# Loading batch 0's queries and keys by halves of the tokens, in sixteen transfers from two queues

## The chip, the core and the metric

One core of a Trainium2 chip runs the whole kernel. Its engines are TensorE (PE in the profile, with its weight loads as PEld), VectorE (DVE), ScalarE (ACT), GpSimd (POOL) and SyncE (SP); the rows SPq are SP's own DMA queue. Transfers between the main memory and the core's on-chip memory are carried out by 16 DMA engines. The metric is the device time of one execution in microseconds (us); of the kernel before there are three such times, and their median counts.

## The reference, cut to what matters

Blockwise causal attention (8 batches, 8 heads, 576 tokens, head size 64; a block of 64 queries sees its own and all earlier key blocks), whose output is the input of a channel mix with a shift by one token:

```python
scores = scale * np.matmul(q, k.transpose(0, 1, 3, 2))
scores = np.where(block_i >= block_j, scores, -1e9)
attn = np.exp(scores - scores.max(-1)); attn /= attn.sum(-1) + 1e-9
x = np.matmul(attn, v).transpose(0, 2, 1, 3).reshape(B, S, H * D)     # 8 x 576 x 512
x_prev = x shifted by one token, zeros first
xk = mu_k * x + (1 - mu_k) * x_prev;  xr = mu_r * x + (1 - mu_r) * x_prev
out = sigmoid(xr @ w_r) * (np.maximum(xk @ w_k, 0) ** 2 @ w_v)        # 512 -> 1024 -> 512
```

## The kernel before, in words

The kernel is written as a list of 958 tasks. Each task belongs to one engine and issues a few instructions. Three hand-held tables set everything: `ORDER` is the order in which all tasks are issued (and so the order on each engine; `+5` behind a number puts five matmuls of 512 columns that nobody reads in front of that PE task, line L256), `PLACE` gives for each task with a choice the engine that does it (A, D or P), and `RINGS` gives the number of buffers of each kind. Engines run their own list in order and wait for each other through semaphores.

The tasks, by the names that the text uses:

- `qkld b g n`: SP loads the queries (n = 0) or keys (n = 1) of four heads (g = 0 or 1) of batch b into one of the six load buffers `t_ld`, 128 x 1152 float32, 576 KB. Heads are numbered 4g + 2x + y. A partition holds nine consecutive tokens of one head of each x; y picks the upper or the lower 64 partitions.
- `qk b g n`: a cast to bf16 into `t_nl` (POOL, DVE or ACT, L247 or L243), which puts the two x side by side.
- `turn b g n`: nine 128 x 128 transposes on PE (L350) into a score buffer `t_s` in PSUM, three of which exist; `ev b g n` copies it to `t_qkt`, where a batch's queries and keys lie with the head size on the partitions.
- `sc b part i`: the matmuls of one score unit (L422), and `ex b part i` its exponential on ACT (L431). Batch 0 is cut in two: part 0 is tokens 0 to 255 with three units, part 1 tokens 256 to 575 with ten. Later batches have twelve units.
- `av b part S` sums the exponentials (L470, L481), `av b part A` and `B` multiply them with the values `t_vo` (L497); then `t1`, `rec`, `t2` and `norm` on DVE divide, `d` (L622) takes the difference to the token before, and `mul` (L639) writes the mixed inputs XK and XR.
- `pk`, `pr`, `pv` are the three matrix products of the channel mix on PE (L686 and, for its first chunk by halves, L706; L731; L760), over nine chunks of 512 tokens. `relu`, `sq`, `tanh` and `o` lie between and behind them, and SP stores.

The channel mix needs the mixed inputs of tokens, and so attention of batch 0 has to be through before the first `pk` can run. Weights go through the same six load buffers: they are loaded behind batch 0's queries and keys. Batches 4 to 7 turn their queries and keys by DMA transposes and are not touched.

Of the kernel before, what the change touches and what calls it, by code (L numbers as in the profile page):

```python
# [21 lines left out]


ORDER = """
# [50 lines left out]
"""  # L75


PLACE = (
    "AAPDAPDADDDAAADADAPDDDDDPPPAPAPAPDDDPDDDAAPAPAAAPPDPPDDAPADDDDDDPD"
    "DPDPAPPPPPPPDPPPPPPPDPDPAADDPDPPAADPPADADPDAADDDDDDAAPDPAPAAAADPAA"  # L80
    "APDPAADPDPAADAAADPDPDDDAADADAPAPAADPDPAAADAPAAADDAADDDDDAPAPAPAPDA"
    "ADAPAPDPAAAADDAPADAPDAADADDDADADADAAAPAPADADADADADADAD"
)


# [67 lines left out]
def kernel(  # L153
# [12 lines left out]
    nc = tc.nc  # L166
    B, H, S, D = q.shape
# [7 lines left out]
    QC = 32  # L175
    JT = S // D
    HALF = S // 2
# [34 lines left out]
    def new(buf):  # L212
        return slots[buf["ring"], buf["slot"]]
# [44 lines left out]
                identb[:, :].unsqueeze(1).to_broadcast([P, 4, P]),  # L258
                start=True, stop=True)

    def load(key, buf, jobs):
        def fn(eng, me):
            for dst, src in jobs(new(buf)):
                nc.sync.dma_start(dst, src)
        return add(key, "SP", fn, uses=[buf])

    cast, ready, evac = {}, {}, {}
    vo_buf = [plan.buf("vo") for _ in range(B)]
    qkt_buf = [plan.buf("qkt") for _ in range(B)]
# [3 lines left out]
    def halves(ld, w):  # L273
        return ld[:, 0:2 * w].rearrange("p (x e) -> p x e", x=2)
# [32 lines left out]
                                 AD if name == "v" else ANY, fn, [t], [ld])  # L307


    def where(n, g, y, lo):  # L310

        return ((g * 2 + n) * 2 + y) * S + lo

    def add_qk(b, g, n):
        src = (q, k)[n]
        ld, nl = plan.buf("ld"), plan.buf("nl")
        cross = b in CROSS
        if cross:
            t = load(f"xld {b} {g} {n}", ld, lambda d: [
                (d[:, :].rearrange("p (t d) -> p t d", d=D),  # L320
                 src[b, 4 * g:4 * g + 4].rearrange(
                     "h s d -> (h s) d").rearrange("(t p) d -> p t d", p=P))])
        else:
            t = load(f"qkld {b} {g} {n}", ld, lambda d: [
                (halves(d, S), src[b, 4 * g:4 * g + 4].rearrange(
                     "(x y) (p j) d -> (y p) x (j d)", y=2, j=JT))])

        def fn(eng, me):
            return convert(
                eng, new(nl)[:, :].rearrange("p (t x d) -> p x t d", x=2, d=D),  # L330
                new(ld)[:, :].rearrange("p (x t d) -> p x t d", x=2, d=D))
        c = add(f"qk {b} {g} {n}", ANY, fn, [t], [ld, nl])
        at = where(n, g, 0, 0)
        if cross:
            def turn(eng, me):
                nc.sync.dma_start_transpose(
                    out=new(qkt_buf[b])[:, at:at + 2 * S].rearrange(
                        "p (t c) -> p t c", c=P),
                    in_=new(nl)[:, 0:2 * S])
            evac[b, g, n] = add(f"xturn {b} {g} {n}", "SP", turn, [c],  # L340
                                [nl, qkt_buf[b]])
            return
        m = plan.buf("s")

        def turn(eng, me):
            unread(me, new(m)[:, 0])
            pst = new(m)[:, :, :].rearrange("p a b -> p (a b)").bitcast(BF)
            for j in range(JT):
                at = slice(j * P, (j + 1) * P)
                nc.tensor.matmul(pst[:, at], new(nl)[:, at], identb,  # L350
                                 is_transpose=True, start=True, stop=True)
        t = add(f"turn {b} {g} {n}", "PE", turn, [c],
                [nl, m, qkt_buf[b]])

        def ev(eng, me):
            pst = new(m)[:, :, :].rearrange("p a b -> p (a b)").bitcast(BF)
            convert(eng, new(qkt_buf[b])[:, at:at + 2 * S].rearrange(
                "q (p j) -> q p j", j=JT),
                pst[:, 0:2 * S].rearrange("q (j p) -> q p j", p=P))
        evac[b, g, n] = add(f"ev {b} {g} {n}", AD, ev, [t],  # L360
                            [m, qkt_buf[b]])

# [43 lines left out]
    def add_scores(key):  # L406
# [6 lines left out]
        def fn(eng, me):  # L413
            qkt, PS = new(qkt_buf[b]), new(m)
            unread(me, PS[:, 0])
            for y, t, col, q0, n in pieces:
                for g in range(2):
                    for x in range(2):
# [4 lines left out]
                            PS[g * D:g * D + D, x, col:col + n],  # L423
                            qkt[rows, ka:ka + D], qkt[rows, qa:qa + n],
                            start=True, stop=True)
        deps = [evac[b, g, n] for g in range(2) for n in range(2)]
        pe = add(f"sc {b} {part} {i}", "PE", fn, deps,
                 [m, qkt_buf[b], ebuf[key]])

# [418 lines left out]
```

## Time and profile before

| | |
|---|---|
| median of three executions | 256.73 us (255.5 to 257.11) |
| profiled execution | 255.6 us, of which the profile's span is 253.3 us |
| busy time in the span | PE 241.4 us, DVE 193.6, ACT 172.4, POOL 83.2 |
| granted TensorE clock | full (9 tenths or more in all 40 slices) |
| chain that ended last | PE 75%, DVE 10%, ACT 7%, DMA 3%, issue 2% |
| moved by DMA | 48.21 MB, 190 GB/s on average |

The profile is of one execution; times in it count from the start of its span. PE's busy time counts the unread matmuls of L256 as well, and pipelined matmuls overlap in it. The chain is followed back from the last instruction to whatever released each step. A view by windows gives the busy time of each engine, the share of time in which the 16 DMA engines were at work, and the bytes that they moved in any stretch.

### The profile page before, as it was taken

What the parts mean: (1) busy time and instruction counts of PE and PEld (TensorE: products, weight loads), DVE (VectorE), ACT (ScalarE), POOL (GpSimd) and SP (SyncE); (2) the same over time, 40 slices, a digit from 0 to 9 for tenths busy, and PEclk for the clock granted to TensorE, in tenths of its full rate; (3) what the DMA queues carried; (4) which work ended last, traced back from release to release, by engine and by line L of the source; (5) the groups of instructions that cost most, each with busy time, mean ns of one, the idle gap of its engine ahead of it and who ended that gap; (6) DMA issues with size and microseconds to landing.
All of it is one profiled execution on the core that took longest, in us unless ns stands there. A gap on an engine that the chain in (4) does not pass through costs nothing.

```text
span 253.3 us, 7859 instructions
## 1 busy us (share of the span) xinstructions
PE 241.4 (95%) x3429; PEld 125.8 (50%) x3429; DVE 193.6 (76%) x274; ACT 172.4 (68%) x228; POOL 83.2 (33%) x74
## 2 busy tenths in 40 slices
PE   4999599999999999999999999999999999999994
PEld 2555474774464444644554455445544554444452
DVE  1348898899999999889836979998798579943532
ACT  3699599989988369558595958597549931450630
POOL 1033523433543453651578001335750043010100
PEclk9999999999999999999999999999999999999999
DMA  7999998999999999999999999979913002203103
GB/s 238 297 290 400 372 284 215 323 270 175 278 260 181 211 231 222 184 215 217 192 225 192 224 229 232 211 196 196 177 44 124 3 3 83 87 0 126 39 21 145
DMA packets 105905, 48.21 MB, mean 190 GB/s; under 512 B 94736, under 2 KB 94992, under 8 KB 105872
## 3 DMA queue, kind: packets, MB, share of 16 engines
q1 hardware_dynamic: 105872, 47.72, 81.1%
q8 instruction: 26, 0.43, 0.7%
q14 instruction: 7, 0.06, 0.1%
HBM read 33.56 MB, written 9.44 MB: 170 GB/s over the span
## 4 chain that ended last, share of the span: by engine, by line
PE 75%; DVE 10%; ACT 7%; DMA 3%; issue 2%; POOL 0%; DVEq 0%; ACTq 0%; POOLq 0%
PE t_mm L760 24%; PE t_mm L686 19%; PE t_mm L731 11%; PE t_s L497 7%; ACT t_e L431 6%; PE t_s L422 6%; PE t_s L481 4%; PE t_s L350 2%; DMA t_ld<-in_moe_w_v_dram 2%; DVE XK L639 2%; PE t_mm L256 2%; DMA t_ld<-in_k_dram 1%; DVE t_xt L595 1%; DVE t_d L622 1%; DVE XR L639 1%
## 5 line engine op out<-in xcount | busy, mean ns | idle before, releaser
L431 ACT ACTIVATE t_e<-t_s 128x1024 f16<-128x1024 f32 (+2 forms) x97 | 87.4, 977 | 10.2 <-PE t_s L422 10.1
L760 PE MATMUL t_mm<-WV,t_k 128*128 128x512 f16 (+1 forms) x296 | 65.8, 374 | 0.1
L686 PE MATMUL t_mm<-XK,WK 128*128 128x512 f16 x256 | 60.3, 379 | 0.4 <-DVE t_kr L666 0.2
L674 POOL TENSOR_TENSOR t_k<-t_kr 128x512 f16<-128x512 f32 x26 | 27.2, 1059 | 72.7 <-DVE t_k L674 31.0
L664 ACT ACTIVATE t_kr<-t_mm 128x512 f32<-128x512 f32 x48 | 28.7, 603 | 24.6 <-PE t_mm L686 23.2
L760 PEld LDWEIGHTS <-t_k 128*128 128x128 f16 x296 | 27.7, 98 | 32.5 <-issue 1.5
L686 PEld LDWEIGHTS <-WK 128*128 128x128 f16 x256 | 23.8, 97 | 30.0 <-issue 4.4
L768 DVE SCALAR_TENSOR_TENSOR t_o<-t_t,t_mm 128x512 f32<-128x512 f32 (+1 forms) x37 | 24.6, 667 | 16.1 <-PE t_mm L760 14.9
L740 ACT ACTIVATE t_t<-t_mm 128x512 f32<-128x512 f32 x36 | 21.6, 606 | 21.0 <-PE t_mm L731 20.7
L731 PE MATMUL t_mm<-WR,XR 128*128 128x512 f16 x144 | 35.6, 380 | 0.1
L639 DVE SCALAR_TENSOR_TENSOR XK<-t_d,MU,t_xt 128x576 f16<-128x576 f32 (+4 forms) x44 | 31.3, 739 | 0.0
L639 DVE SCALAR_TENSOR_TENSOR XR<-t_d,MU,t_xt 128x576 f16<-128x576 f32 (+4 forms) x44 | 31.0, 725 | 0.0
L422 PE MATMUL t_s<-t_qkt 64*64 64x64 bf16 (+7 forms) x672 | 29.1, 284 | 0.8 <-ACT t_e L431 0.4
L622 POOL TENSOR_TENSOR t_d<-t_xt 128x1152 f32<-128x1152 f32 (+1 forms) x10 | 19.3, 1937 | 24.7 <-DVE t_xt L595 13.3
L247 POOL CAST t_nl<-t_ld 128x1152 bf16<-128x1152 f32 x14 | 15.9, 1144 | 33.2 <-DMA t_ld<-in_k_dram 14.3
L674 DVE TENSOR_TENSOR t_k<-t_kr 128x512 f16<-128x512 f32 x27 | 19.3, 726 | 9.6 <-ACT t_kr L664 9.2
L497 PE MATMUL t_s<-t_e,t_vo 64*32 64x320 f16 (+7 forms) x1344 | 23.8, 278 | 2.4 <-issue 2.3
L422 PEld LDWEIGHTS <-t_qkt 64*64 64x64 bf16 x672 | 15.3, 106 | 19.5 <-issue 16.0
L247 POOL CAST t_vo<-t_ld 64x1152 f16<-64x1152 f32 x16 | 18.5, 1154 | 19.8 <-DVE t_d L622 8.1
L497 PEld LDWEIGHTS <-t_vo 64*32 64x32 f16 x1344 | 17.9, 92 | 9.9 <-issue 5.2
L666 DVE TENSOR_SCALAR t_kr<-t_mm 128x512 f32<-128x512 f32 x24 | 16.2, 686 | 6.7 <-PE t_mm L686 6.4
L731 PEld LDWEIGHTS <-XR 128*128 128x128 f16 x144 | 13.2, 98 | 15.3 <-issue 1.3
(44 smaller groups left out, 197.4 us busy)
## 6 DMA issues: line engine op xcount, KB each, us to landing
t_ld<-in_k_dram SPq DMA_DIRECT2D x16, 576.0 KB, 7.1
t_ld<-in_q_dram SPq DMA_DIRECT2D x16, 576.0 KB, 6.4
t_ld<-in_v_dram SPq DMA_DIRECT2D x16, 576.0 KB, 7.4
out_dram<-t_o SPq DMA_DIRECT2D x35, 256.0 KB, 2.4
t_ld<-in_moe_w_k_dram SPq DMA_DIRECT2D x4, 512.0 KB, 7.9
t_ld<-in_moe_w_v_dram SPq DMA_DIRECT2D x4, 512.0 KB, 5.5
t_ld<-in_moe_w_r_dram SPq DMA_DIRECT2D x2, 512.0 KB, 6.8
t_qkt<-t_nl SPq DMA_TRANSPOSE x16, 4.5
```

What stands on the lines that cost most here:

```text
L247: return e.tensor_copy(dst, src)
L422: nc.tensor.matmul(PS[g * D:g * D + D, x, col:col + n], qkt[rows, ka:ka + D], qkt[rows, qa:qa + n], start=True, stop=True)
L431: nc.scalar.activation(new(ebuf[key])[:, :, 0:width], new(m)[:, :, 0:width], AF.Exp, scale=ISQ)
L497: nc.tensor.matmul(dst(slice(c * QC, (c + 1) * QC), u, f, q0, n), weights(b, u, c, t, f), new(ebuf[key])[u * D:u * D + D, x, col:col + n], ...
L622: return e.tensor_tensor(new(d)[:, 0:2 * n].rearrange("p (u t) -> p u t", u=2), x[:, :, 1 + lo:1 + hi], x[:, :, lo:hi], ALU.subtract)
L639: return nc.vector.scalar_tensor_tensor((XK, XR)[kr][:, cc, g:g + w], new(d)[:, u * n + at - lo:u * n + at - lo + w], MU1[:, kr, cc:cc + 1 ...
L664: nc.scalar.activation(new(kr), new(m), AF.Relu)
L674: return e.tensor_tensor(dst(), KR, KR, ALU.mult)
L686: nc.tensor.matmul(ps, WK[:, cc, jc * P:(jc + 1) * P], XK[:, cc, at:at + CH], start=(cc == 0), stop=(cc == CCn - 1))
L731: nc.tensor.matmul(ps, XR[:, cc, g % R:g % R + P], WR[:, cc], start=(cc == 0), stop=(cc == CCn - 1))
L760: nc.tensor.matmul(ps[:, 0:w], k2[:, jc, jt * P:(jt + 1) * P], WV[:, jc, cols], start=(jc == 0), stop=(jc == JCn - 1))
L768: nc.vector.scalar_tensor_tensor(new(o)[:, 0:w], new(tb)[:, cols], 1.0, new(m)[:, 0:w], ALU.add, ALU.mult)
```

## The change

For batch 0 alone, n is now a half of the tokens (n = 0: tokens 0 to 287, n = 1: 288 to 575), and one load buffer holds both tensors: queries in partitions 0 to 63, keys in 64 to 127. A buffer is filled by four transfers: for each pair of heads x and each tensor one, with 64 destination partitions of 2,304 bytes. Their source is two heads y, 36,864 elements apart, with 32 runs of 576 elements each. The n = 0 buffers take the two tensors by two queues (queries from SP, keys from ACT), the n = 1 buffers all from SP. The cast and the nine transposes stay as they were; the copy behind the transposes spreads its columns over the four places (queries and keys, y = 0 and 1). The three score units of part 0 wait for the two n = 0 copies only; part 1 waits for all four. `ORDER` and `PLACE` are new throughout; the unread matmuls are 25 instead of 33.

```diff
 ORDER = """
-26 34 22 30 0 41 27 28+5 35 29 36+2 37 23 24+4 25 116 31 38 1 32+4 33 76+5
+30 22 34 31 26 32+5 23 38 33 24+2 25 35 48+5 44 41 49 36 27 45 46 37 47 28+1
...
-    def load(key, buf, jobs):
+    def load(key, buf, jobs, also=None):
         def fn(eng, me):
-            for dst, src in jobs(new(buf)):
-                nc.sync.dma_start(dst, src)
+            for n, (dst, src) in enumerate(jobs(new(buf))):
+                (nc.sync if n % 2 == 0 or also is None else also).dma_start(
+                    dst, src)
         return add(key, "SP", fn, uses=[buf])
...
-        else:
+        elif b:
             t = load(f"qkld {b} {g} {n}", ld, lambda d: [
                 (halves(d, S), src[b, 4 * g:4 * g + 4].rearrange(
                     "(x y) (p j) d -> (y p) x (j d)", y=2, j=JT))])
+        else:
+            t = load(f"qkld {b} {g} {n}", ld, lambda d: [
+                (halves(d, S)[i * D:(i + 1) * D, x],
+                 a[0, 4 * g + 2 * x:4 * g + 2 * x + 2,
+                   n * HALF:(n + 1) * HALF].rearrange(
+                       "y (r j) d -> y r (j d)", j=JT))
+                for x in range(2) for i, a in enumerate((q, k))],
+                None if n else nc.scalar)
...
         def ev(eng, me):
             pst = new(m)[:, :, :].rearrange("p a b -> p (a b)").bitcast(BF)
+            if not b:
+                convert(eng, new(qkt_buf[0])[:, g * 4 * S:(g + 1) * 4 * S]
+                        .rearrange("q (a t) -> q a t", a=4)[
+                            :, :, n * HALF:(n + 1) * HALF].rearrange(
+                                "q a (r j) -> q a r j", j=JT),
+                        pst[:, 0:2 * S].rearrange(
+                            "q (j a r) -> q a r j", a=4, r=QC))
+                return
...
-        deps = [evac[b, g, n] for g in range(2) for n in range(2)]
+        deps = [evac[b, g, n] for g in range(2)
+                for n in range(1 if (b, part) == (0, 0) else 2)]
```

SP's queue at the program's start, before; `t_ld_58` to `t_ld_63` are the six load buffers:

```order
L264 DMA t_ld_58<-in_k_dram 128x2x576
L264 DMA t_ld_59<-in_k_dram 128x2x576
L264 DMA t_ld_60<-in_q_dram 128x2x576
L264 DMA t_ld_61<-in_q_dram 128x2x576
L279 DMA MU<-in_moe_mu_k_dram 128x2x2
L279 DMA MU<-in_moe_mu_r_dram 128x2x2
L264 DMA t_ld_62<-in_v_dram 128x18x64
L264 DMA t_ld_63<-in_k_dram 128x2x576
```

The same place after, with the semaphores that an issue waits for; DMAHW0 to DMAHW7 are the eight semaphores that transfers count up when they have landed, given out in turn to SP's and ACT's transfers:

```order
L264 DMA t_ld_58<-in_q_dram 64x1x576 x2
L264 DMA t_ld_59<-in_q_dram 64x1x576 x2
L264 DMA t_ld_60<-in_q_dram 64x1x576 [waits DMAHW0_49]
L264 DMA t_ld_60<-in_k_dram 64x1x576 [waits DMAHW1_49]
L264 DMA t_ld_60<-in_q_dram 64x1x576 [waits DMAHW2_49]
L264 DMA t_ld_60<-in_k_dram 64x1x576 [waits DMAHW3_49]
L264 DMA t_ld_61<-in_q_dram 64x1x576 [waits DMAHW4_49]
L264 DMA t_ld_61<-in_k_dram 64x1x576 [waits DMAHW5_49]
L264 DMA t_ld_61<-in_q_dram 64x1x576 [waits DMAHW6_49]
L264 DMA t_ld_61<-in_k_dram 64x1x576 [waits DMAHW7_49]
L264 DMA t_ld_62<-in_v_dram 128x18x64 [waits DMAHW0_49]
L264 DMA t_ld_63<-in_v_dram 128x18x64 [waits DMAHW1_49]
```

Four loads of all 128 partitions have become twelve transfers here (and four more on ACT); from the ninth transfer on, each issue waits until an earlier one has landed, and the values, mu and everything else stand behind them.

ACT at the program's start, before (`t_s_150` to `t_s_152` are the three score buffers, `t_e` the exponentials):

```order
L243 ACT_TABLE_LOAD
L243 CAST t_nl_67<-t_ld_58 128x2x9x64
L243 COPY t_qkt_74<-t_s_150 128x1152
L243 COPY t_qkt_74<-t_s_151 128x1152
L243 COPY t_qkt_74<-t_s_152 128x1152
L431 ACTIVATE t_e_84<-t_s_151 128x1024
L431 ACTIVATE t_e_86<-t_s_150 128x1024
L431 ACTIVATE t_e_87<-t_s_151 128x2x256
```

And after:

```order
L264 DMA t_ld_58<-in_k_dram 64x1x576 x2
L264 DMA t_ld_59<-in_k_dram 64x1x576 x2
L243 ACT_TABLE_LOAD
L243 COPY t_qkt_74<-t_s_151 128x4x288
L452 ACTIVATE t_e_84<-t_s_152 128x2x256
L452 ACTIVATE t_e_85<-t_s_150 128x1024
L452 ACTIVATE t_e_86<-t_s_152 128x1024
L243 CAST t_vo_79<-t_ld_62 64x18x64
L452 ACTIVATE t_e_87<-t_s_151 128x1024
```

ACT issues four of the transfers first, does one of the four copies instead of all of them, and has the three exponentials of part 0 ahead of the values' cast and the ten of part 1.

More of the change, by code (lines that the diff above doesn't have):

```diff
@@ L24 @@
 ORDER = """
[50 rows of a table removed]
[50 rows of a table added]
 """
 PLACE = (
[L79 to L82, printed above, removed]
+    "APAPPPAADADADDPDDDADDDDPDDPAPADDAADPPDDPDAPAAAAADAPPDDPDPAPADAAADA"
+    "PPDPAADAADDPDPPDAPAADPDPAAADAPPDDDDPPPDPDPDAADADDDAAADADDPDPDADPDP"
+    "DADDDDDDAPAPDDADAPAPDAAADADPDAAAAPAADADDADDDADAPDAADDDDAADDPADDPDP"
+    "DPADDPDPDPDPDPDADDDDAAADADADADADAPADADADAPADAPADADADAD"
 )
```

98 rows, old and new, of the table ORDER are left out of this document.

## The prediction

> **What bounds the kernel now.** I read the page first, then the windows, the chain in order of time, the timeline of the first 40 us, and the DMA views of the same stretch. The page says that PE is busy nearly throughout and closes the chain:
>
> ```profile
> PE 241.4 (95%) x3429; PEld 125.8 (50%) x3429; DVE 193.6 (76%) x274; ACT 172.4 (68%) x228; POOL 83.2 (33%) x74
> PE 75%; DVE 10%; ACT 7%; DMA 3%; issue 2%; POOL 0%; DVEq 0%; ACTq 0%; POOLq 0%
> ```
>
> The windows say where PE is not the bound. First three rows of all instructions, then two of the unread matmuls of L256 alone (columns: stretch, length, PE busy, PEld busy, and so on, DMA share and GB/s last):
>
> ```profile
> 20.00:30.00 10.00, 6.34 (x224) 4.26 (x223) 8.29 (x18) 7.21 (x9) 3.69 (x4) 1.00 1.04 394
> 30.00:40.00 10.00, 9.80 (x187) 6.83 (x185) 9.23 (x17) 9.59 (x12) 2.97 (x3) 1.00 1.09 276
> 120.00:240.00 120.00, 120.00 (x1544) 58.43 (x1543) 91.90 (x125) 75.85 (x108) 38.51 (x30) 1.00 0.64 137
> 0.00:10.00 10.00, 5.09 (x11) 1.41 (x11) 1.00 0.83 264
> 10.00:20.00 10.00, 5.01 (x19) 1.45 (x19) 1.00 1.13 299
> ```
>
> From 30 us on PE has work all the time; from 120 to 240 it is busy in all of it. Before 30 us half of PE's busy time is unread matmuls, and from 20 to 30 it stands 3.7 us. So the kernel is a start of 30 us, set by batch 0, and then a stretch in which PE works off a fixed list. Whatever moves the end of the start moves the end of the kernel by as much, less what PE has done ahead. The start is read in the timeline:
>
> ```profile
> 4.28 1.15 ACT L243 CAST t_nl<-t_ld 128x1152 bf16<-128x1152 f32 x1 [2.27 <-DMA t_ld<-in_k_dram]
> 9.99 0.76 DVE L247 CAST t_nl<-t_ld 128x1152 bf16<-128x1152 f32 x1 [1.02 <-DMA t_ld<-in_q_dram]
> 11.16 0.67 PE L350 MATMUL t_s<-identb,t_nl 128*128 128x128 bf16 x9
> 11.86 1.12 ACT L243 COPY t_qkt<-t_s 128x1152 bf16<-128x1152 bf16 x1 [0.25 <-PE t_s L350]
> 12.83 1.05 PE L422 MATMUL t_s<-t_qkt 64*64 64x320 bf16 x32
> 13.47 10.63 ACT L431 ACTIVATE t_e<-t_s 128x1024 f16<-128x1024 f32 x13 [0.49 <-PE t_s L422]
> 30.21 1.04 PE L706 MATMUL t_mm<-XK,WK 128*128 128x256 f16 x8
> ```
>
> The first cast starts when the first load has landed (4.28), the last when the fourth has (9.99). 2.84 us later the first scores run, then 13 exponentials back to back until 24.10, and the first `pk` at 30.21. The loads come at the speed of the DMA engines, all 16 busy:
>
> ```profile
> 0.00:2.30 2.30, 1.00 0.17 26
> 2.30:10.00 7.70, 5.88 (x32) 3.21 (x31) 1.53 (x3) 3.39 (x3) 0.00 (x0) 1.00 1.02 335
> 2.30:4.30 2.00, 1.38 (x4) 0.19 (x2) 0.00 (x0) 0.02 (x1) 0.00 (x0) 1.00 1.00 385
> 20.00:25.00 5.00, 4.53 (x170) 2.92 (x169) 3.85 (x7) 4.95 (x7) 2.19 (x2) 1.00 1.05 395
> ```
>
> Nothing flows before 2.3 us; then a DMA share of 1.00 to 1.05 goes with 335 to 395 GB/s, that is 20.9 to 24.7 GB/s for one engine of 16.
>
> **The change, part by part.**
>
> *The bytes* are the same: 16 transfers of 64 runs of 2,304 bytes are 2.36 MB, as four loads of 576 KB.
>
> *On how many engines they run* decides all. Each load of before had an outermost count of 128 on the on-chip side, and its source could be merged into evenly spaced rows: 64 rows of 576 elements are just the 36,864 elements from one head to the next. The new source cannot: 32 runs cover 18,432 elements, then the next head starts 36,864 after the first. So its outermost count is two. If a transfer is dealt to the engines by its outermost count, as 128 rows fall into 16 equal shares, there are only two shares here. If the 2 x 32 runs are counted as 64 first, there are 16. No row of before shows a transfer with such a source; the ends are 2 engines and 16. I take 2, because the pattern as it stands has no even stride over its 64 runs, and all rows that show 16 belong to patterns that do.
>
> The Trainium skill, DMA: Bandwidth & Descriptors, section "Why a DMA increments its semaphore by 16 and not by 1", says the same more sharply: the engines used are the largest number up to 16 that divides the outermost count (not 1) of both patterns, and the lowest-numbered ones, for SP and ACT alike; counts of 2 and 64 give two. No run here shows it yet. The page's 27 GiB/s for one engine would give, as an estimate, 41 us for the 2.36 MB and 285 us in all by the sum below.
>
> *The price by two engines.* 24.4 GB/s (385 to 395 over 16) times two is 48.8 GB/s, and 2.36 MB take 48.4 us: the last lands at 2.3 + 48.4 = 50.7 us. The n = 0 buffers, half of the bytes, land by 26.5. Issuing does not add to it: an issue takes about half a microsecond of SP,
>
> ```profile
> 0.73 0.97 SPq L264 DMA_DIRECT2D t_ld<-in_k_dram  x2
> L264 SPq DMA_DIRECT2D t_ld<-in_moe_w_k_dram x4: 545/551/3450, 10.6 to 20.1; - x4
> ```
>
> and transfers nine to sixteen wait for the first eight, while those keep the two engines busy. Behind them on SP's queue stand the values, mu, batch 1's loads and, through the six buffers, the weights. Their shares on the two engines lie behind the small transfers too, so all of them come late by about the same.
>
> *Behind the last landing* comes the old tail: 2.84 us to the scores, with one difference, the copy on DVE instead of ACT (+0.24):
>
> ```profile
> L247 DVE COPY t_qkt<-t_s 128x1152 bf16<-128x1152 bf16 x3 | 4.0, 1348 | 3.6 <-PE t_s L350 3.6
> L243 ACT COPY t_qkt<-t_s 128x1152 bf16<-128x1152 bf16 x13 | 14.3, 1120 | 6.8 <-PE t_s L350 6.8
> ```
>
> So part 1's scores run at 50.7 + 2.84 + 0.24 = 53.8, and its exponentials from 54.4 (0.64 later, as at 12.83 and 13.47). The new copy has more dimensions; I price it as the old one, since it is as many elements with the same stride, and twice its time would add 1.35.
>
> *What the split gains:* part 0's three exponentials are done in the wait for n = 1. They are 2,560 of 11,520 columns, so 2.4 of the 10.63 us. The ten others take 8.3 and end at 62.7, against 24.10 before: 38.6 later.
>
> *To the first `pk`* it was 6.1 us from there. Now ACT has, behind the ten, a copy, a cast, two copies and a weight cast to do:
>
> ```profile
> L243 ACT CAST t_nl<-t_ld 128x1152 bf16<-128x1152 f32 x8 | 9.1, 1157 | 5.0 <-DMA t_ld<-in_k_dram 4.5 <-issue 0.5
> L243 ACT CAST WK<-t_ld 128x1024 f16<-128x1024 f32 x2 | 2.1, 1046 | 0.4 <-DMA t_ld<-in_moe_w_k_dram 0.4
> ```
>
> 3 x 1.12 + 1.16 + 1.05 = 5.6, so `pk` at 68.3, 38.1 later. By then PE has done one turn and two score units of batch 1 more than at 30.21 (0.5 and 0.35 each in the chain):
>
> ```profile
> 71.94 0.50 PE t_s L350 x9
> 43.74 0.37 PE t_s L422 x4
> ```
>
> That is 1.2 us of its fixed list. The eight unread matmuls that were dropped lay in idle time and give nothing.
>
> *The rest of the order.* Ten `relu`, seven `sq`, three casts, two copies and three `d` go to DVE, some casts leave it; by the order's counts and the rows' durations that is some 15 us more on DVE and as much less on POOL:
>
> ```profile
> L666 DVE TENSOR_SCALAR t_kr<-t_mm 128x512 f32<-128x512 f32 x24 | 16.2, 686 | 6.7 <-PE t_mm L686 6.4 <-PE t_mm L706 0.2
> L674 DVE TENSOR_TENSOR t_k<-t_kr 128x512 f16<-128x512 f32 x27 | 19.3, 726 | 9.6 <-ACT t_kr L664 9.2
> 40.00:60.00 20.00, 19.17 (x375) 12.22 (x377) 17.27 (x24) 17.80 (x23) 8.75 (x8) 1.00 1.00 267
> 60.00:90.00 30.00, 29.49 (x436) 15.17 (x428) 28.46 (x35) 22.49 (x30) 11.90 (x10) 1.00 1.14 221
> ```
>
> PE's bound hides it while DVE has room: 28 us are free in 120 to 240, only 4.3 in 40 to 90. If half of it fell in there, 3.3 us would stick out. I take 0 and keep 3 for the range.
>
> *Sum:* 38.1 - 1.2 = 36.9 on the profiled execution's 255.6, 292.5. That execution is 1.1 below the median of the three, 256.73, within their spread of 1.6. I forecast **293 us**.
>
> Its own range: at 20.9 GB/s an engine the last lands at 58.7, 8 later; at the fastest slice of the loads, 430 GB/s over 16 or 26.9 an engine, at 46.2, 4.5 earlier:
>
> ```profile
> GB/s 0 0 0 0 0 0 146 131 338 399 392 422 400 399 430 369 376 284 215 307 361 399 384 392 392 307 353 363 223 187 196 246 290 286 286 237 212 166 187 338
> ```
>
> That is 288 to 301, with 3 to 4 for the order 285 to 305.
>
> **The rivals.**
>
> *Sixteen engines after all (not slower).* Place: the first transfers; the mechanism is a deal over 64 runs. The first buffer lands near 4.3, the second near 6; SP issues n = 1 after that, four and four at 0.55 each, and the last lands near 11.3 (8.9 for the last issue, 2.4 for a quarter of the first load's bytes). That is 39.4 before my 50.7: 253.5 us, faster by 1.2%. For it: weights with differing patterns on both sides run at 395 GB/s. Against it: their counts divide by 16 on both sides. It decides where the last lands before 50.7 - 36.9 = 13.8, at 205 GB/s, eight or nine engines.
>
> *Each queue on two engines of its own.* Then SP's and ACT's n = 0 transfers run beside each other and land by 14.4; the eight of n = 1, all SP's, take 24.2 more: 38.6, 12.1 earlier than forecast, 281 us. For it: two queues; against it: nothing in the trace shows queues that own engines, since with SP alone all 16 were busy.
>
> The Trainium skill, same page, "Issuing engines are not separate DMA queues", says that a second issuing engine saves only issue time; no run here shows it yet.
>
> *Sixteen engines, but DVE binds* where it was nearly full, from 40 to 90: 253.5 + 3.3 = 257, no change. For it the window rows; against it that the work comes from POOL, which is idle two thirds of the span, so that the new order need not put it into that stretch.
>
> **How the numbers follow.** Two engines 0.83, four 0.05, sixteen 0.09, sixteen with DVE bound 0.03. The likeliest gives 293. For 8 in 10 I go from 279, which takes in the four engines, to 306. 1%, 2.6 us, is about what a measurement of this kernel can tell from no change: the first two cases are slower; sixteen engines is mostly over 1% faster, and DVE's case within it. Faster 0.07, same 0.05, slower 0.88.
>
> **What would show it.** Right: a low DMA share (about 0.13) and some 50 GB/s until about 50 us; the first cast at about 14 us, not 4; part 0's exponentials near 30 us, part 1's not before 54; PE with long waits up to 68 us and full from there. Wrong: a DMA share near 1.0 with over 300 GB/s in the first 10 us, and exponentials of part 0 at 9 to 10 us; then the whole sum falls. If the transfers are slow but the end is far from 293, the rate of an engine or the later order was mis-sized, which the windows behind the first `pk` would tell.

## The result, and the profile after

| | before | after |
|---|---|---|
| median of four executions each | 256.36 us (255.5 to 257.11) | 293.65 us (292.52 to 294.78) |
| profiled execution, and its span | 255.6 us, 253.3 | 293.86 us, 291.1 |
| first `pk` in the profile | 30.21 us | 68.69 us |

The ratio of the times is 1.1456, 95% interval 1.1396 to 1.1516. The forecast was 293 us, with a range of 279 to 306. The times below leave out an execution that lies over 1.5% above the fastest of the same kernel; there was one such, 261.33 us in the run with one transfer for each head.

The page of the profile after: busy times; the granted clock, the DMA share and the GB/s in 40 slices of 7.3 us each; and the chain by engine.

```profile
PE 243.3 (84%) x3421; PEld 125.3 (43%) x3421; DVE 203.7 (70%) x292; ACT 173.5 (60%) x222; POOL 68.8 (24%) x62
PEclk9999855799999999999999999999999999999999
DMA  0111141999969999999989899999997600111103
GB/s 30 52 51 51 52 112 54 237 378 311 314 223 329 263 305 196 214 225 178 236 177 263 160 183 239 199 152 240 207 219 145 189 3 2 74 72 72 72 6 140
PE 66%; SPq 12%; ACT 6%; DMA 6%; DVE 4%; issue 4%; POOL 1%; POOLq 0%; DVEq 0%; ACTq 0%
```

PE is busy 243.3 us, 1.9 more than before, in a span that is 37.8 longer: nearly all the new time is standing time. SP's queue and the DMAs, the latter 3% of the chain before, have 18% of it. The DMA row does not rise above 1 tenth in the first five slices, to 36 us, where the rate stays at 30 to 52 GB/s.

Windows of the profile after (stretch, length, busy time of PE, PEld, DVE, ACT and POOL, granted clock, DMA share, GB/s):

```profile
2.30:10.00 7.70, 1.37 (x4) 0.18 (x2) 0.00 (x0) 1.28 (x1) 0.00 (x0) 1.00 0.13 46
10.00:20.00 10.00, 1.93 (x11) 1.09 (x11) 0.00 (x0) 0.00 (x0) 1.14 (x1) 1.00 0.13 51
30.00:40.00 10.00, 2.31 (x31) 1.29 (x29) 0.76 (x1) 1.51 (x2) 0.00 (x0) 0.71 0.13 52
40.00:50.00 10.00, 1.24 (x15) 0.47 (x13) 0.00 (x0) 1.02 (x1) 0.00 (x0) 0.50 0.44 99
60.00:70.00 10.00, 8.46 (x210) 5.82 (x208) 9.82 (x19) 9.77 (x11) 3.37 (x4) 1.00 1.02 369
70.00:291.00 221.00, 216.20 (x2996) 109.97 (x2988) 182.91 (x255) 152.71 (x200) 62.48 (x51) 1.00 0.81 177
```

The first 7.7 us of the loads, which had a DMA share of 1.02 and 335 GB/s, have 0.13 and 46. 0.13 is two engines of 16, and it stays there to 40 us. From 40 to 50 the values come in beside them, and from 60 to 70, with the weights and batch 1, it is 1.02 and 369 GB/s. The last 221 us of the kernel before, for the last row:

```profile
32.00:253.00 221.00, 216.58 (x3002) 110.68 (x3000) 177.30 (x240) 150.14 (x205) 74.80 (x61) 1.00 0.80 172
```

PE does 0.4 us less in it, DVE 5.6 more, POOL 12.3 less. So the new order left the late part as long as it was: the lost time is all in the start.

The start in the timeline of the profile after (start, duration, engine, line, operation; in brackets the idle time before and what ended it):

```profile
0.73 12.51 SPq L264 DMA_DIRECT2D t_ld<-in_q_dram  x5
16.87 1.14 POOL L247 CAST t_nl<-t_ld 128x1152 bf16<-128x1152 f32 x1 [15.57 <-DMA t_ld<-in_q_dram]
18.07 1.14 PE L360 MATMUL t_s<-identb,t_nl 128*128 128x128 bf16 x9 [14.40 <-POOL t_nl L247]
26.70 0.76 DVE L247 CAST t_nl<-t_ld 128x1152 bf16<-128x1152 f32 x1 [25.45 <-DMA t_ld<-in_q_dram]
27.38 1.35 DVE L247 COPY t_qkt<-t_s 128x1152 bf16<-128x1152 bf16 x1
31.14 1.51 ACT L452 ACTIVATE t_e<-t_s 128x512 f16<-128x512 f32 x2 [1.32 <-PE t_s L441]
38.17 0.76 DVE L247 CAST t_nl<-t_ld 128x1152 bf16<-128x1152 f32 x1 [9.44 <-DMA t_ld<-in_k_dram]
40.76 1.02 ACT L452 ACTIVATE t_e<-t_s 128x1024 f16<-128x1024 f32 x1 [8.10 <-PE t_s L441]
50.52 0.76 DVE L247 CAST t_nl<-t_ld 128x1152 bf16<-128x1152 f32 x1 [11.59 <-DMA t_ld<-in_k_dram]
55.06 8.21 ACT L452 ACTIVATE t_e<-t_s 128x1024 f16<-128x1024 f32 x10 [1.56 <-PE t_s L441]
68.69 1.05 PE L727 MATMUL t_mm<-XK,WK 128*128 128x256 f16 x8 [0.33 <-ACT WK L243]
```

Each of the four casts ends an idle time of its engine of 9 to 25 us, with a transfer as what ended it. The fourth can start at 50.52, against 9.99 before. From there to the first `pk` it is 18.2 us, against 20.2 before, with three of the exponentials already done.

### The profile page after: what moved, and what is told of

It is laid out like the page before. It is cut to its first block, busy times and chain, and to the rows that moved or that the text cites. A ratio compares the mean times of both kernels' runs of the same rounds, so it can differ in the third digit from the quotient of the medians.

```text
span 291.1 us, 7877 instructions
## 1 busy us (share of the span) xinstructions
PE 243.3 (84%) x3421; PEld 125.3 (43%) x3421; DVE 203.7 (70%) x292; ACT 173.5 (60%) x222; POOL 68.8 (24%) x62
## 4 chain that ended last, share of the span: by engine, by line
PE 66%; SPq 12%; ACT 6%; DMA 6%; DVE 4%; issue 4%; POOL 1%; POOLq 0%; DVEq 0%; ACTq 0%
PE t_mm L707 20%; PE t_mm L781 19%; SPq L264 12%; PE t_mm L752 9%; PE t_s L441 6%; PE t_s L518 6%; DMA t_ld<-in_k_dram 5%; ACT t_e L452 4%; PE t_s L502 3%; PE t_s L360 2%; POOL t_nl L247 1%; ACT t_qkt L243 1%; DVE t_k L695 1%; ACT WK L243 1%; ACT t_vo L243 1%
## 5 line engine op out<-in xcount | busy, mean ns | idle before, releaser
L452 ACT ACTIVATE t_e<-t_s 128x1024 f16<-128x1024 f32 (+3 forms) x97 | 87.0, 972 | 16.4 <-PE t_s L441 15.9
L360 PE MATMUL t_s<-identb,t_nl 128*128 128x128 bf16 x144 | 12.4, 242 | 40.9 <-DVE t_nl L247 25.2
L247 DVE CAST t_nl<-t_ld 128x1152 bf16<-128x1152 f32 x13 | 10.0, 767 | 46.9 <-DMA t_ld<-in_q_dram 25.5
L685 ACT ACTIVATE t_kr<-t_mm 128x512 f32<-128x512 f32 x38 | 22.7, 604 | 23.8 <-PE t_mm L707 23.3
L695 DVE TENSOR_TENSOR t_k<-t_kr 128x512 f16<-128x512 f32 x34 | 24.8, 733 | 10.9 <-ACT t_kr L685 10.4
L441 PE MATMUL t_s<-t_qkt 64*64 64x320 bf16 (+7 forms) x672 | 29.4, 287 | 1.3 <-ACT t_e L452 0.5
L360 PEld LDWEIGHTS <-t_nl 128*128 128x128 bf16 x144 | 10.0, 109 | 45.9 <-DVE t_nl L247 26.8
L243 ACT COPY t_qkt<-t_s 128x1152 bf16<-128x1152 bf16 x11 | 12.5, 1146 | 25.7 <-PE t_s L360 25.7
L687 DVE TENSOR_SCALAR t_kr<-t_mm 128x512 f32<-128x512 f32 x34 | 22.9, 685 | 5.6 <-PE t_mm L707 4.7
L441 PEld LDWEIGHTS <-t_qkt 64*64 64x64 bf16 x672 | 15.2, 108 | 20.2 <-issue 16.4
L518 PE MATMUL t_s<-t_e,t_vo 64*32 64x64 f16 (+7 forms) x1344 | 23.6, 278 | 0.0
```

The lines of the kernel that those rows point to most:

```text
L247: return e.tensor_copy(dst, src)
L360: nc.tensor.matmul(pst[:, at], new(nl)[:, at], identb, is_transpose=True, start=True, stop=True)
L441: nc.tensor.matmul(PS[g * D:g * D + D, x, col:col + n], qkt[rows, ka:ka + D], qkt[rows, qa:qa + n], start=True, stop=True)
L452: nc.scalar.activation(new(ebuf[key])[:, :, 0:width], new(m)[:, :, 0:width], AF.Exp, scale=ISQ)
L518: nc.tensor.matmul(dst(slice(c * QC, (c + 1) * QC), u, f, q0, n), weights(b, u, c, t, f), new(ebuf[key])[u * D:u * D + D, x, col:col + n], ...
L695: return e.tensor_tensor(dst(), KR, KR, ALU.mult)
```

## The experiments

The outermost count is the size of the first dimension of a transfer's access pattern. The theory was that a transfer is dealt out by it, to as many engines and no more (16 at most), and that this count, two heads, was all that cost the time. The rivals: engines counted over the 64 runs, with the slowness from something else (the number of transfers, their half of the partitions, the new order, two queues that share a place). Each diff below is against the changed kernel unless it says otherwise.

### Only the order of the loops in the source

```diff
-                       "y (r j) d -> y r (j d)", j=JT))
+                       "y (r j) d -> r y (j d)", j=JT))
```

The partitions then alternate between the two heads, and the copy behind the transposes sorts the columns accordingly. The 16 transfers, their sizes, partitions and queues stay.

> The changed kernel with one thing turned round: the source of each of the 16 transfers is written with its 32 runs outermost and the two heads inside (32 x 2 x 576 instead of 2 x 32 x 576), and the copy behind the transposes puts the columns back in place. Same bytes, same 16 transfers of 64 partitions, same queues, same order. Theory (a transfer runs on as many engines as its outermost count lets it, so 2 before and 16 now): the DMA share is near 1.0 in the first 10 us, the last half lands at about 11, not 50, and the time is 252 to 257 us. Rival (small transfers into 64 partitions are slow as such): nothing changes, 293 us. Rival (the new order is what costs the time): the loads land early, but the time stays above 285 us.

255.22 us (254.31 to 256.91, nine executions); ratio to the kernel before 0.9952, 0.992 to 0.9984. A window, and four rows of the timeline:

```profile
2.30:10.00 7.70, 4.04 (x24) 2.31 (x23) 2.05 (x2) 1.28 (x1) 1.14 (x1) 1.00 1.01 268
```

```profile
6.14 1.14 POOL L247 CAST t_nl<-t_ld 128x1152 bf16<-128x1152 f32 x1 [4.83 <-DMA t_ld<-in_q_dram]
12.51 0.76 DVE L247 CAST t_nl<-t_ld 128x1152 bf16<-128x1152 f32 x1 [1.58 <-DMA t_ld<-in_k_dram]
16.31 8.21 ACT L452 ACTIVATE t_e<-t_s 128x1024 f16<-128x1024 f32 x10 [0.19 <-PE t_s L441]
30.07 1.05 PE L727 MATMUL t_mm<-XK,WK 128*128 128x256 f16 x8 [0.33 <-ACT WK L243]
```

The DMA share is 1.01 instead of 0.13, the last cast comes 38.0 us earlier, the first `pk` 38.6, and the end 38.4 (by the medians). With the outermost count at 32, the loss is gone, whole. The number of transfers, the half partitions, the queues and the new order are all still there, so none of them made it. The last cast is 1.5 us later than the expected 11: SP's last issue ends only at 9.1 us.

### The smallest pair: adjacent heads, and heads that lie apart

Here the 16 transfers are replaced by eight of all 128 partitions, from two heads each. In the one kernel the two are neighbours, so that the source merges into 128 evenly spaced rows; in the other a head lies between them, and it keeps an outermost count of two. Nothing else differs.

```diff
+                (halves(d, S)[:, i],
+                 a[0, 4 * g + 2 * n:4 * g + 2 * n + 2].rearrange(     # adjacent
+                       "h (p j) d -> (h p) (j d)", j=JT))
```
```diff
+                 a[0, 4 * g + n:4 * g + n + 3:2].rearrange(           # apart
+                       "h (p j) d -> h p (j d)", j=JT))
```

> A probe of loading alone: the changed kernel with 8 transfers of 128 partitions instead of 16 of 64; each takes all tokens of two neighbouring heads, whose 128 runs are evenly spaced, so that the outermost count is 128. The buffers then hold other heads than the rest of the kernel takes them for (the scores are of shuffled data); bytes, order and all other work are the same. Theory: 16 engines, the last lands at about 10, 251 to 256 us. Both rivals on the loads agree; the rival that blames the new order says above 285 us.

> The same probe with one difference: each of the 8 transfers takes two heads that are not neighbours (every second one), so that their 2 x 64 runs are not evenly spaced and the outermost count is 2. Size, partitions, number of transfers and run length are those of the probe with neighbours, and the scores are of shuffled data here too. Theory (outermost count): 2 engines, about 50 GB/s, last landing at about 50, 290 to 296 us. Rival (small transfers into 64 partitions): like the probe with neighbours, 251 to 256 us.

One execution each: 253.47 us adjacent, 293.2 us apart. The same window, first adjacent, then apart:

```profile
2.30:10.00 7.70, 5.47 (x28) 2.91 (x27) 3.54 (x4) 1.75 (x2) 1.14 (x1) 1.00 1.07 352
```

```profile
2.30:10.00 7.70, 1.37 (x4) 0.19 (x2) 0.00 (x0) 1.28 (x1) 0.00 (x0) 1.00 0.13 45
```

The same bytes in the same number of transfers of the same shape run at 352 GB/s or at 45, by which two heads they take. 39.7 us hang on it. It is not that every second head is slow to read: the third form of the source, below, reads every second head too, with 32 outermost, at a DMA share of 1.03 and 1.04 in the same window.

### Four and eight heads outermost

```diff
+                 a[0, 4 * g:4 * g + 4, n * HALF:(n + 1) * HALF].rearrange(            # four
+                       "h (r j) d -> h r (j d)", j=JT))
```
```diff
+                 a[0, :, (2 * n + g) * 144:(2 * n + g + 1) * 144].rearrange(          # eight
+                       "h (r j) d -> h r (j d)", j=JT))
```

> The probe of loading with 8 transfers of 128 partitions, whose source is now four heads with 32 runs each (the tokens of one half), so that the outermost count is 4; the buffers hold other heads than the kernel takes them for, bytes and order are the same. Theory (as many engines as the outermost count): 4 engines, about 100 GB/s and a DMA share of 0.25 until the last lands, at 2.3 + 24.2 = 26.5 us, some 24 earlier than with two heads apart; the time is 268 to 272 us. Rival (any source without an even stride is slow, whatever its count): 293 us.

> The same probe with eight heads of 16 runs each, an outermost count of 8 (shuffled data again). Theory: 8 engines, about 200 GB/s and a DMA share of 0.5, last landing at 2.3 + 12.1 = 14.4 us, time 256 to 260 us, so close to no change against the kernel before. Rival (any source without an even stride is slow): 293 us.

One execution each: 270.97 us with four, 259.33 us with eight. A window and the last cast, with four heads:

```profile
2.30:10.00 7.70, 1.38 (x4) 0.19 (x2) 0.00 (x0) 1.28 (x1) 0.00 (x0) 1.00 0.24 89
```

```profile
27.96 0.76 DVE L247 CAST t_nl<-t_ld 128x1152 bf16<-128x1152 f32 x1 [4.80 <-DMA t_ld<-in_k_dram]
```

And with eight:

```profile
2.30:10.00 7.70, 3.22 (x15) 1.28 (x13) 0.00 (x0) 1.28 (x1) 1.14 (x1) 1.00 0.71 199
```

```profile
17.06 0.76 DVE L247 CAST t_nl<-t_ld 128x1152 bf16<-128x1152 f32 x1 [2.41 <-DMA t_ld<-in_k_dram]
```

Four outermost give a share of 0.24, close to four sixteenths. With eight, it is 0.48 from 2.3 to 5.4 us, close to eight sixteenths. The eight transfers have been issued by 4.9 us, the values are issued from 5.4, and from 7 to 11 us they lift the share to 0.93 and more, which makes the 0.71 of the row. In both the last cast comes later than 2.36 MB by so many engines would need (1.5 and 2.7 us later than expected). The values' loads, which bring the share to that of 16 engines, are by then in flight and take a part of the same ones; that is read from the traces and was not tried by itself. Ordered by the last cast, the runs read:

| outermost count | last cast (us) | time (us) |
|---|---|---|
| 2 (apart) | 49.91 | 293.2 |
| 4 | 27.96 | 270.97 |
| 8 | 17.06 | 259.33 |
| 32, loops swapped | 12.51 | 255.22 |

From two to four the cast moves by 22.0 us and the time by 22.2; from four to eight by 10.9 and 11.6. A microsecond of landing is about a microsecond of kernel. The rows with 2, 4 and 8 are of one execution each.

### No outermost heads at all: one transfer for each head

```diff
+                (halves(d, S)[i * D + y * QC:i * D + (y + 1) * QC, x],
+                 a[0, 4 * g + 2 * x + y, n * HALF:(n + 1) * HALF].rearrange(
+                       "(r j) d -> r (j d)", j=JT))
+                for x in range(2) for y in range(2)
```

> The changed kernel with each transfer cut into one per head: 32 transfers of 32 runs into 32 partitions, 72 KB each, with an outermost count of 32. Theory (outermost count): 16 engines; the issues take over as the limit (24 on SP at about 0.45 us, with waits for the transfers before), the last half lands at 12 to 15, and the time is 254 to 259 us. Rival (small transfers into few partitions): half the size, half the partitions and twice the number must be worse, over 293 us. Rival (the new order): above 285 us.

258.5 us (257.41 to 259.3, nine executions); ratio 1.0065, 1.0041 to 1.0089.

```profile
2.30:10.00 7.70, 4.96 (x27) 2.52 (x26) 2.03 (x2) 1.81 (x2) 1.14 (x1) 1.00 0.71 206
```

And from its timeline two issues in a row and the last cast:

```profile
8.92 0.42 SPq L264 DMA_DIRECT2D t_ld<-in_k_dram  x1
9.38 0.42 SPq L264 DMA_DIRECT2D t_ld<-in_q_dram  x1
...
14.75 0.76 DVE L247 CAST t_nl<-t_ld 128x1152 bf16<-128x1152 f32 x1 [2.99 <-DMA t_ld<-in_k_dram]
```

32 transfers of 72 KB remove nearly all of the loss, but the DMA share stays at 0.71. SP issues one in 0.46 us without a pause, which feeds 160 GB/s, and once ACT's eight have been issued (at 5.4 us) that is what flows: 169 GB/s from 6 to 10 us and 159 from 10 to 13, at a share of 0.59 and 0.57. So issuing, which cost nothing in the change, now holds the engines back, and the last cast comes at 14.75 and not at 12.51.

### The old order with good loads

The loads are those with the loops swapped; `ORDER` and `PLACE` are those of the kernel before. This order also has the n = 1 halves issued first: SP issues their eight transfers ahead of its part of n = 0.

```diff
-30 22 34 31 26 32+5 23 38 33 24+2 25 35 48+5 44 41 49 36 27 45 46 37 47 28+1
+26 34 22 30 0 41 27 28+5 35 29 36+2 37 23 24+4 25 116 31 38 1 32+4 33 76+5
```

> The loads by halves with 32 runs outermost (16 engines), but with the old order and the old placing of all tasks. There the first scores are of part 1 and wait for all four copies, so the halves open nothing earlier, while the loads land later than four whole ones (12.5 instead of 10 us). Theory (once all 16 engines run, what the halves bring is only that part 0's scores start early, which needs the new order): 257 to 260 us, slower than the same loads in the new order (255.2). Rival (order and placing do not matter): 255 us, the same as with the new order.

261.99 us (261.59 to 262.35, four executions); ratio 1.0185, 1.0168 to 1.0202, two above the upper end of what was expected.

```profile
8.08 1.28 ACT L243 ACT_TABLE_LOAD   x1 [8.08 <-DMA t_ld<-in_k_dram]
9.38 1.15 ACT L243 CAST t_nl<-t_ld 128x1152 bf16<-128x1152 f32 x1
18.11 10.62 ACT L452 ACTIVATE t_e<-t_s 128x1024 f16<-128x1024 f32 x13 [0.50 <-PE t_s L441]
```

By these rows the miss lies with ACT, which the old order gives the first cast, here of an n = 1 half. ACT waited for the transfer until 8.08, then loaded its table, and cast at 9.38, where the cast stood at 4.28 before: 5.1 later. Turns and copies follow it one by one as before, so that the exponentials begin 4.6 later (18.11 and 13.47). All 13 run in one row: nothing in this order uses that part 0 needs one half only. The last cast stands at 13.13, not far from the 12.51 in the new order. Between the two orders with the same transfers lie 6.8 us (261.99 and 255.22), so the split needs the new one; how much of this is the order of the loads and how much that of the tasks behind them was not separated.

### How many queues

These three use a third form of the source, in which the two x lie inside the rows on both sides, so that both patterns have the same three dimensions. The first keeps the queues of the change, the second issues everything from SP, the third all keys from ACT (the last two lines of the diff are for the second; the third has `nc.scalar` there, the first keeps the line).

```diff
-                (halves(d, S)[i * D:(i + 1) * D, x],
-                 a[0, 4 * g + 2 * x:4 * g + 2 * x + 2,
+                (halves(d, S)[i * D + y * QC:i * D + (y + 1) * QC],
+                 a[0, 4 * g + y:4 * g + y + 3:2,
                    n * HALF:(n + 1) * HALF].rearrange(
-                       "y (r j) d -> y r (j d)", j=JT))
-                for x in range(2) for i, a in enumerate((q, k))],
+                       "x (r j) d -> r x (j d)", j=JT))
+                for y in range(2) for i, a in enumerate((q, k))],
-                None if n else nc.scalar)
+                None)                    # all by SP; nc.scalar: both queues for all
```

> The better version with the queues of the change: 16 transfers of 32 x 2 x 576 on both sides, keys of n = 0 by ACT, all of n = 1 by SP. It differs from the version with both queues in four issues (the keys of n = 1), and from the one with 32 runs outermost in the form of the transfers. Theory (16 engines, then the issues of SP decide): between the two, 253.8 to 255 us; the form alone gives under 1 us. Rival (the second queue brings nothing beyond issue time that is hidden anyway): 253.7 us, the same as with both queues.

> The same 16 transfers, all issued by SP. Theory: 16 issues of about 0.45 us in a row, the last not before 8 us, n = 0's second buffer some 1 to 2 us later than with two queues; 255 to 257 us. If the second queue gave engines of its own, the loads would be at half speed here and the time over 260 us.

> An attempt at a better version: 16 transfers again, but one per tensor and y, with 32 partitions and the two x side by side (32 x 2 x 576 on both sides), so that the outermost count is 32 and the copy behind the transposes stays that of the change; and the keys of both halves are issued by ACT, those of the queries by SP. Theory: 16 engines and half the issues on SP; n = 1 lands at 10 to 11 instead of 12.5 and the time is 253 to 254.5 us, faster than the kernel before by about 1%. If the second queue brings nothing, 255 us as with all of n = 1 on SP.

| | time (us) | ratio to before |
|---|---|---|
| queues of the change | 254.33 (253.8 to 255.68, six) | 0.9903, 0.9867 to 0.9938 |
| SP alone | 254.92 (253.99 to 255.28, six) | 0.9933, 0.9909 to 0.9957 |
| keys by ACT throughout | 253.73 (253.47 to 254.7, four) | 0.9876, 0.9853 to 0.9898 |

Timeline with SP alone, the first of its issues and the last:

```profile
0.73 0.40 SPq L264 DMA_DIRECT2D t_ld<-in_q_dram  x1
7.75 0.42 SPq L264 DMA_DIRECT2D t_ld<-in_k_dram  x1
```

Timeline of the kernel with the keys by ACT, which beats both kernels, and below it its window:

```profile
0.73 6.76 ACTq L264 DMA_DIRECT2D t_ld<-in_k_dram  x8
0.73 6.53 SPq L264 DMA_DIRECT2D t_ld<-in_q_dram  x8
15.54 8.21 ACT L452 ACTIVATE t_e<-t_s 128x1024 f16<-128x1024 f32 x10 [0.29 <-PE t_s L441]
29.31 1.05 PE L727 MATMUL t_mm<-XK,WK 128*128 128x256 f16 x8 [0.33 <-ACT WK L243]
```

```profile
2.30:10.00 7.70, 5.17 (x27) 2.57 (x26) 2.65 (x3) 1.94 (x2) 1.14 (x1) 1.00 1.04 298
```

All three load by 16 engines: the share from 2.3 to 10 us is 1.03, 0.90 and 1.04. By the medians the second queue is worth 0.6 to 1.2 us. The intervals of the first two overlap, so the 0.6 is not shown; those of the last two just don't, but they come from different sets of executions, with 256.54 and 256.83 us for the kernel before. Smaller expectations were missed: SP alone is 0.1 us below its range, its second cast is 0.2 us later than with the queues of the change (7.77 and 7.58) and not 1 to 2, and with the keys by ACT the last cast stands at 11.74 and not at 10 to 11.

With the keys by ACT the last issue ends at 7.5 us instead of 8.2 with SP alone, and the median is 3.1 us or 1.2% below that of the kernel before. Between the two profiled executions (253.9 and 255.6) it is 1.7: the first `pk` comes 0.9 us earlier, from there to the end of the span it is 0.3 less (222.8 and 223.1), and outside the span 0.5 less (1.8 and 2.3).

## Why the prediction was right, step by step

**Two engines.** Right, and shown by the swapped loops, the pair and the row of counts. The Trainium skill, DMA: Bandwidth & Descriptors, "Why a DMA increments its semaphore by 16 and not by 1", has it as the largest number up to 16 that divides both outermost counts. The shares 0.13 at two, 0.24 at four and 1.01 at 32 agree; a small count was tried on the source's side alone. Which engines a small count gets, of which the section also speaks, no run here showed.

**The rate.** 24.4 GB/s an engine was taken; 51 to 52 GB/s over two are 25.5 to 26.0. The first stretch, at 46, is a little slower, and the last landing fits: 50.52 against 50.7. By the Trainium skill's 27 GiB/s the estimate was 285 us, some 9 below the measured time: the rate of the trace was the better price. The row in which nothing was said to flow before 2.3 us has 26 GB/s, which is 0.06 of the 2.36 MB and changes nothing.

**The first cast.** It came at 16.87, not at about 14. The prediction let the second n = 0 buffer land at 26.5, which it did (26.70), but gave the first buffer half of that time. Transfers of both buffers were in flight at once, eight of them from two queues, so the first had to share the two engines with the second; that reading was not tested. It cost nothing, since the last landing decides.

**Part 0's exponentials near 30 us.** Two of three: 31.14, and the third at 40.76. Its scores stand on PE behind the turn of the third buffer, whose cast came at 38.17. The step overlooked what stands ahead on PE's list. It cost nothing either, as part 1 came later still.

**The tail.** Scores were to run 3.1 us behind the landing and the exponentials from 54.4 to 62.7; the scores ran 3.9 us behind the fourth cast's start, and the exponentials from 55.06 to 63.27. Two steps were mis-sized. The turn took 1.14 us, 0.47 more than the fourth turn of before by which it was priced, though it started 0.35 sooner behind its cast (0.82 and 1.17). From its end to the scores it was 2.0 us, against 1.0 before and 0.24 more for the copy. The copy took 1.35 on DVE, as priced, and ended at 53.95; but PE's list has the sums of part 0 and three unread matmuls there, which end at 54.53:

```profile
52.41 0.72 PE L491 MATMUL t_mm<-t_e,pick 128*32 128x256 f16 x16
53.07 1.46 PE L256 MATMUL t_mm<-identb 128*128 128x512 bf16 x3
54.46 0.90 PE L441 MATMUL t_s<-t_qkt 64*64 64x320 bf16 x20
```

`pk` came at 68.69 instead of 68.3.

**Work done ahead and the later order.** 1.2 us were to be regained; from `pk` to the end of the span it is 222.4 us after and 223.1 before, so 0.7. DVE has 10.1 us more and not 15, and PE's bound hid them, as the 70 to 291 row shows. (By the prediction's own figures the 3.3 us that might stick out are 3.2.) The new order was taken as nothing; here, with the start so late, that holds. With good loads the order with halves is worth something: 253.73 to 255.22 against 256.5 to 256.8 before.

**The sum.** 36.9 us was forecast on 255.6; 293.86 less 255.6 is 38.3. The 1.4 are the late `pk` (0.4), 0.5 less regained, and 0.5 more outside the span (2.8 and 2.3).

**The rivals.** Sixteen engines would have given 253.5: the runs that kept 16 engines busy, or nearly (a share of 0.90 or more from 2.3 to 10 us), gave 253.47 to 255.22 with the new order, so the price was right and the condition wrong. The break-even was put at eight or nine engines; eight gave 259.33, 1% above before, so it lies somewhat higher; in that run the values were in flight beside the last transfers. Queues with engines of their own fall: with SP's and ACT's transfers in flight the rate was 46 to 51, with SP's alone 52. The Trainium skill, same page, "Issuing engines are not separate DMA queues", agrees: a second issuer saved 0.6 to 1.2 us by the medians here, and the 0.6 is within the noise.

## What to carry to other kernels

Before splitting a load, look at the outermost dimension that is left in its source. Here counts of 32 and 128 ran on all 16 engines, and counts of 2, 4 and 8 on as many engines as they say. Where two or four heads would stand outermost, swap the loops, and sort the columns later where a copy is done anyway. A DMA share that stands at two or four sixteenths while engines wait is the sign of it. Where one engine works off a fixed list, price a changed start by its last landing alone, one for one.

## What the runs showed of the hardware that was not expected

The granted TensorE clock fell to 0.71 from 30 to 40 us and to 0.50 from 40 to 50, where PE was busy for 2.31 and 1.24 of 10 us; from 10 to 20 us, with 1.93, it was still full. Before, with unread matmuls in the shorter waits, it was full throughout. It did not set the time: executions with a mean clock of 0.963 to 0.964 took 292.52 to 293.86 us, and one with 1.0 took 294.78. Nor does the column tell what a turn takes. The one at 18.07 took 1.14 us at a clock of 1.00, and so did the first of the kernel before:

```profile
5.49 1.14 PE L350 MATMUL t_s<-identb,t_nl 128*128 128x128 bf16 x9 [1.82 <-ACT t_nl L243]
```

The fourth took 0.67 there. What makes the difference stays open.

An issue on SP took 0.40 to 0.43 us where both sides have the same three dimensions (SP alone, above), and 0.60 with the loops swapped, where the source has one more, in the timeline of that run:

```profile
8.51 0.60 SPq L264 DMA_DIRECT2D t_ld<-in_k_dram  x1
```

The number of dimensions is not all of it: with adjacent heads both sides have two, and single issues took 0.43 to 0.62. Behind slow transfers an issue is far longer: 12.51 us for SP's first five after the change, of which the fifth has a landing to wait for. The pair of heads tells the two apart, since its eight transfers are too few for any to wait for a landing. SP's first three issues, first with adjacent heads, then with heads apart:

```profile
0.73 1.34 SPq L264 DMA_DIRECT2D t_ld<-in_q_dram  x3
```

```profile
0.73 12.76 SPq L264 DMA_DIRECT2D t_ld<-in_q_dram  x3
```

So an issue itself takes longer while the transfers run on two engines; what holds it is not shown.
